# Attention in groups of 64 keys over two pairs of heads, all in 64x64 tiles, with part of the queries and keys turned by VectorE

## The chip, the cores and the metric

The kernel runs on one core of a Trainium2 chip. The metric is the device time of one execution in microseconds; the time before is the median of three runs.

The engines are called as the profile calls them: PE is TensorE's matmuls and PEld its weight loads, DVE is VectorE, ACT is ScalarE, POOL is GpSimd and SP is SyncE, which here issues most DMAs.

## The reference

The kernel computes a normalized attention and, on its output, an MLP mixer. All is float32 but the mixer's weights, which arrive as float64. Cut to what matters:

```python
# q, k, v: (8, 12, 448, 64)
q_n = q / sqrt(mean(q*q, -1) + 1e-6) * g_q        # k_n likewise, with g_k
scores = q_n @ k_n.T / sqrt(64)
attn = exp(scores - max(scores))
attn = attn / (sum(attn) + 1e-9)
x = heads_side_by_side(attn @ v)                   # (8, 448, 768)
h = relu(x.T @ w_tok1) @ w_tok2                    # 448 -> 256 -> 448, over tokens
u = x + h.T
out = u + relu(u @ w_ch1) @ w_ch2                  # 768 -> 1536 -> 768, over channels
```

## The kernel before

**Elements and pairs.** The batch has eight elements of twelve heads. Two heads make a pair `p`; an element has six pairs (`NPAIR`), and there are 48 in all. A pair fills 128 partitions: one head in rows 0 to 63 and the other in rows 64 to 127.

**One program order.** Every engine executes its instructions in the order in which the Python code emits them. That order is made by `merge` (L27), which interleaves lists of (cost, function) items so that each list advances at the same share of its total cost. An item of cost 0.0 is placed as soon as its list's turn comes, and occupies no share. While the mixer of element `b` runs (`tok1`, `tok2`, `ch1`, `ch2`), the attention of element `b + 1` is merged into it. Element 0's attention runs first, merged with the conversion of the mixer's weights to float32 (`weight_items`), most of which VectorE does. Element 0's mixer uses plain products (`ch1_first`, `ch2_first`, L713 and L731); the other elements use seven products in place of eight per block of the channel matmuls (`ch1` L750, `ch2` L807). These seven products combine block sums of the operands, and the sums of the weights are made once, by `sum_items`.

**Steps of the attention.** `att_step(g)` emits one step; four steps, s = 0 to 3, take two pairs `p` and `p + 1` through. A step's attention matmuls are one item (`tiled`), about which the other items of the step are placed.

- `score` (L321) takes a chunk of 128 keys of one pair. Two matmuls with a 64x128 stationary tile, one per head, lie in the upper and the lower half of the array.
- `score_last` (L335) takes the last 64 keys of both pairs in four 64x64 tiles. 448 keys are three chunks of 128 and this one.
- ScalarE then takes the exponential (L311). The factor of the key's norm is the activation's per-partition scale, so that only queries have to be scaled beforehand.
- `av` (L422) multiplies a chunk by the values, with 128x64 tiles, and `av_last` (L434) does it for the last keys in 64x64 tiles.
- The softmax sums: for element 0, matmuls with a matrix of ones (`ones`, L401) accompany each chunk. From element 1 on, `chunk_sums` adds the chunks up first (the first sum on POOL, L382; the others on VectorE, L388 and L393), and `row_sums` makes one pass of `ones` per pair.
- `denominator` turns the sums, takes the reciprocal, turns back and scales the output (L463 to L469, all VectorE).

**Preparing queries and keys.** `load_qk` (L1034, L1036, L1040) loads a pair into one of three buffers of `qk_t` (element 0's go to a larger area). `squares` (ScalarE L1057, VectorE L1061 and L1065) and `roots` with `rsqrt` (VectorE, L1090 to L1095) give the reciprocal norms, `swap` (L346) copies one of them to the other half of the partitions, and `scale` (L291) scales the queries, on VectorE for elements 0 and 1 and on POOL after that. `trans_qk` turns queries and keys by TensorE (L301, four transposes each) and ScalarE multiplies by g while copying out of PSUM (L303). The keys of a pair p + 4 are loaded at step 1 of pair p, those of p + 5 at step 3; their squares follow at steps 0 and 1 of pair p + 2.

**Buffers.** PSUM has four buffers for scores, transposes and row sums (`ps_S`), two for attention outputs (`ps_O`) and two for the mixer's products (`ps_M`, called m_ps). `e_pool` has four buffers for exponentials, `es_pool` one for their sums, `qkT_pool` two for turned pairs, `unit_pool` six for units of mixer weights, which SP loads in the order of use (L676).

Of the kernel before, what the change touches and what calls it, by code (L numbers as in the profile page):

```python
# [8 lines left out]
F32 = mybir.dt.float32  # L9
# [35 lines left out]
def whole(ctx, tc, shifted, pre, q, k, v, g_q, g_k, moe_w_tok1, moe_w_tok2, moe_w_ch1, moe_w_ch2, out):  # L45
# [11 lines left out]
    NS = 4  # L57
# [13 lines left out]
    K3 = NS - 1  # L71
    assert S == K3 * P + D and NPAIR % 2 == 0
# [7 lines left out]
    pre.st_pool = pool("st_pool", 4)  # L80
    pre.nt_pool = pool("nt_pool", 2)
    qkT_pool = pool("qkT_pool", 2)
# [181 lines left out]

    def heads(p):
        return pre.heads(p)

    def load_v(p):
        b, hs = heads(p)
        st["v", p] = vt = pre.v_t[p % 2]  # L270
        nc.sync.dma_start(
            out=vt[:, 0:2 * K3 * D].rearrange("p (h f) -> p h f", h=2),
            in_=v[b, hs, 0:K3 * P].rearrange("h (p c) d -> p h (c d)", c=K3))
        for a in range(2):
            nc.sync.dma_start(out=vt[last_rows(p, a), 2 * K3 * D:], in_=v[b, hs][a][K3 * P:S])

    def last_rows(p, a):

        return slice((a ^ p % 2) * D, (a ^ p % 2) * D + D)

    def scale(p, eng=nc.gpsimd):

        n = 2 * NS
        qk, rs = st["qk", p], st["rs", p]
        parts = [(R, 0, n, rs[0:R, 0:n].unsqueeze(2))]
        if shifted:
            parts.append((P, n, n - 2, rs[:, n:2 * n - 2].unsqueeze(2)))
            parts.append((P, 2 * n - 2, 2, rs[:, 2 * n - 2:2 * n - 1].unsqueeze(2)))
        for rows, o, m, r in parts:
            x = qk[0:rows, o * D:(o + m) * D].rearrange("p (r d) -> p r d", d=D)  # L290
            eng.tensor_tensor(out=x, in0=x, in1=r.to_broadcast([rows, m, D]), op=ALU.mult)  # L291

    def trans_qk(p, i):
        qk = st["qk", p]
        if ("qkT", p) not in st:
            st["qkT", p] = qkT_pool.tile([P, S + NS * P], F32, name="qkT")
        ps = s_tile("t_ps")
        n = P if i else R
        for c in range(NS):
            o = (i * NS + c) * P  # L300
            nc.tensor.transpose(ps[:, c * n:(c + 1) * n], qk[0:n, o:o + P], ident[0:n, 0:n])  # L301
        to = st["qkT", p][:, S:S + NS * P] if i else st["qkT", p][:, 0:S]
        nc.scalar.mul(to, ps[:, 0:NS * n], g_t[:, i:i + 1])  # L303
        if p and i == 1 or p == 0 and i == 0:
            st.pop(("qk", p))
# [4 lines left out]
    def exp(out, ps, p, r):  # L310
        nc.scalar.activation(  # L311
            out=out, in_=ps[:, 0:S], func=AF.Exp, scale=st["rs", p][:, r:r + 1])

    def score(p, kc):

        qkT = st["qkT", p]
        e = st["e", p, kc] = e_tile()
        pss = [s_tile("s_ps") for a in range(2)]
        for a in range(2):
            o = S + kc * P  # L320
            nc.tensor.matmul(  # L321
                out=pss[a][:, 0:S], lhsT=qkT[a * D:(a + 1) * D, o:o + P],
                rhs=qkT[a * D:(a + 1) * D, 0:S], start=True, stop=True)
        for a in range(2):
            exp(e[:, a, :], pss[a], p, 2 * NS + kc * 2 + a)

    def score_last(p):

        e = e_tile()
        pss = [s_tile("s_ps") for i in range(2)]  # L330
        for i in range(2):
            qkT = st["qkT", p + i]
            for a in range(2):
                o = S + K3 * P + a * D
                nc.tensor.matmul(  # L335
                    out=pss[i][last_rows(p + i, a), 0:S], lhsT=qkT[a * D:(a + 1) * D, o:o + D],
                    rhs=qkT[a * D:(a + 1) * D, 0:S], start=True, stop=True)
        for i in range(2):
            exp(e[:, i, :], pss[i], p + i, 4 * NS - 2 + i)
            st["e", p + i, K3] = e  # L340

    def swap(p):

        rs = st["rs", p]
        for a in range(2):
            nc.vector.tensor_copy(  # L346
                out=rs[last_rows(p, a), 4 * NS - 1:4 * NS], in_=rs[a * D:(a + 1) * D, 4 * NS - 2:4 * NS - 1])

    def score_shifted(p):

        qT, kT = st["qkT", p][:, 0:S], st["qkT", p][:, S:S + NS * P]
        for kc in range(NS):
            st["e", p, kc] = e_tile()
        for c in range(NS):
            for a in range(2):
                ps = s_tile("s_ps")
                last = K3 * P + a * D
                for o, k in ((0, kT[a * D:(a + 1) * D, 0:K3 * P]), (K3 * P, kT[a * D:(a + 1) * D, last:last + D])):
                    nc.tensor.matmul(
                        out=ps[0:R, o:o + k.shape[-1]], lhsT=qT[a * D:(a + 1) * D, c * R:(c + 1) * R],  # L360
                        rhs=k, start=True, stop=True)
# [5 lines left out]
                pt = s_tile("p_ps")  # L367
                r = last_rows(p, a)
                for kc in range(NS):

                    k = eq[0:R, kc * P - (r.start if kc == K3 else 0):min(S, (kc + 1) * P)]
                    nc.tensor.transpose(pt[0:k.shape[-1], kc * R:(kc + 1) * R], k, ident[0:R, 0:R])
                for kc in range(NS):
# [791 lines left out]
```

## Time and profile before

| what | value |
|---|---|
| median of 3 runs | 1432.62 us (1427.3 to 1433.27) |
| the profiled execution, its own time | 1438.43 us |
| its span in the profile | 1436.3 us |
| PE busy | 1368.3 us, 95% |
| DVE busy | 726.7 us, 51% |
| ACT busy | 431.2 us, 30% |
| POOL busy | 423.6 us, 29% |
| mean share of the DMA queue q1 / q10 | 56.6% / 5.1% |
| mean granted clock of TensorE | 0.978 |

Busy times come from one profiled execution, so sums are made against its own time, 1438.43 us, and not against the median. A row of the timeline gives the start in us from the start of the span, the duration in us, engine, line, operation, what is written and read, shapes and the number of records merged into the row. Matmuls are pipelined: a row's duration reaches into the next one's, and the time that a group costs is the difference between its start and the next group's start. A number in brackets is idle time of the engine, with what ended it.

### The profile page before, as it was taken

To read this page: it belongs to the slowest core of one execution; us is meant where nothing else is said; L and a number is where in the kernel's file an instruction comes from. 1 tells how busy PE (TensorE), PEld (TensorE's weight loads), DVE (VectorE), ACT (ScalarE), POOL (GpSimd) and SP (SyncE) were. 2 spreads that over 40 slices of the span, in tenths; PEclk is the share of its full clock that TensorE was granted. 3 is DMA by queue.
4 is the path that set the end of the run, shared out by engine and by line. 5 is a ranking of instruction groups with operands and counts; after the bars stand their busy time and mean duration, and the time that the engine had idled before them with its cause. 6 is when DMAs were issued, how large, how long until landed. Compare 5 with 4: busy or idle time off the path is not lost.

```text
span 1436.3 us, 18872 instructions
## 1 busy us (share of the span) xinstructions
PE 1368.3 (95%) x6472; PEld 960.4 (67%) x6472; DVE 726.7 (51%) x1336; ACT 431.2 (30%) x779; POOL 423.6 (29%) x425
## 2 busy tenths in 40 slices
PE   6988996999999999999999999999999999999997
PEld 2333442446776867785777867786777857876997
DVE  7779888225463355644445354633556444432312
ACT  5565453203432043312333033312333134310100
POOL 1122323336664033221233123421323123311320
PEclk9899998999999999999999999999999999999999
DMA  7557777785887934666456744667356744457455
GB/s 176 142 178 201 221 206 181 201 217 141 233 260 219 225 95 136 169 159 156 130 142 177 184 112 133 152 185 173 101 146 177 179 114 142 130 144 172 144 175 119
DMA packets 408301, 238.76 MB, mean 166 GB/s; under 512 B 274500, under 2 KB 366788, under 8 KB 408196
## 3 DMA queue, kind: packets, MB, share of 16 engines
q1 hardware_dynamic: 318178, 226.24, 56.6%
q10 hardware_dynamic: 89890, 11.22, 5.1%
q8 instruction: 54, 0.88, 0.3%
q14 instruction: 51, 0.42, 0.1%
q0 software_dynamic: 128, 0.00, 0.0%
HBM read 197.85 MB, written 39.52 MB: 165 GB/s over the span
## 4 chain that ended last, share of the span: by engine, by line
PE 77%; DMA 7%; DVE 5%; issue 1%; SPq 1%; ACT 1%; ACTq 1%; POOL 0%; DVEq 0%; POOLq 0%
PE m_ps L750 24%; PE m_ps L807 20%; PE s_ps L321 7%; PE o_ps L422 7%; PE m_ps L628 5%; PE m_ps L620 3%; DMA unit<-ws 3%; PE m_ps L731 3%; PE d_ps L401 2%; PE t_ps L301 2%; PE m_ps L713 2%; DMA out_dram<-turned 1%; DMA xs<-turned 1%; PE o_ps L434 1%; DVE raw L213 1%
## 5 line engine op out<-in xcount | busy, mean ns | idle before, releaser
L807 PE MATMUL m_ps<-hb,unit 128*128 128x224 f32 x1764 | 347.1, 356 | 6.8 <-DMA unit<-ws 6.8
L807 PEld LDWEIGHTS m_ps<-hb,unit 128*128 128x128 f32 x1764 | 332.0, 191 | 23.5 <-issue 11.3
L311 ACT ACTIVATE e<-s_ps,rs 128x448 f32<-128x448 f32 x336 | 186.9, 634 | 195.2 <-PE s_ps L321 163.0
L750 PE MATMUL m_ps<-tu,unit 128*128 128x224 f32 x1008 | 202.9, 355 | 0.0
L750 PEld LDWEIGHTS m_ps<-tu,unit 128*128 128x128 f32 x1008 | 187.5, 190 | 16.2 <-issue 4.9
L750 PE MATMUL m_ps<-uT,unit 128*128 128x224 f32 x756 | 152.8, 355 | 0.0
L321 PE MATMUL s_ps<-qkT 64*128 64x448 f32 x576 | 142.8, 595 | 7.8 <-ACT qkT L303 5.7
L750 PEld LDWEIGHTS m_ps<-uT,unit 128*128 128x128 f32 x756 | 141.2, 190 | 13.1 <-issue 12.2
L422 PE MATMUL o_ps<-e,v 128*64 128x448 f32 x576 | 132.3, 563 | 0.0
L816 POOL TENSOR_TENSOR uT<-uT,r 128x448 f32<-128x448 f32 (+1 forms) x56 | 52.7, 952 | 235.9 <-DVE r L816 140.5
L388 DVE TENSOR_TENSOR es<-es,e 128x896 f32<-128x896 f32 x42 | 53.2, 1268 | 117.4 <-ACT e L311 74.6
L463 DVE STREAM_TRANSPOSE dt<-d_ps 128x448 f32<-128x448 f32 x42 | 27.3, 650 | 168.0 <-PE d_ps L401 168.0
L291 POOL TENSOR_TENSOR qk_t<-qk_t,rs 112x512 f32<-112x512 f32 x36 | 37.4, 1060 | 226.1 <-DVE rs L1095 166.1
L321 PEld LDWEIGHTS s_ps<-qkT 64*128 64x128 f32 x576 | 51.3, 193 | 74.9 <-issue 57.6
L382 POOL TENSOR_TENSOR es<-e 128x896 f32<-128x896 f32 x42 | 89.8, 2138 | 32.5 <-ACT sq L1057 29.0
L816 DVE TENSOR_TENSOR uT<-uT,m_ps 128x448 f32<-128x448 f32 (+1 forms) x70 | 34.1, 503 | 124.8 <-PE m_ps L807 124.8
L620 PE MATMUL m_ps<-x,w_sb 112*128 112x384 f32 x256 | 90.9, 508 | 5.6 <-DMA x<-xs 3.4
L303 ACT ACTIVATE qkT<-t_ps,g_t 128x448 f32<-128x448 f32 (+1 forms) x96 | 60.2, 661 | 109.9 <-PE t_ps L301 109.9
L422 PEld LDWEIGHTS o_ps<-e,v 128*64 128x64 f32 x576 | 33.1, 137 | 87.4 <-issue 85.8
L246 POOL TENSOR_TENSOR stage<-raw 128x512 f32<-128x512 f32 x36 | 41.4, 1151 | 146.6 <-DVE raw L232 78.8
L628 PE MATMUL m_ps<-w_sb,h 128*128 128x448 f32 x192 | 78.5, 558 | 4.8 <-DVE uT L633 4.8
L620 PEld LDWEIGHTS m_ps<-x,w_sb 112*128 112x128 f32 x256 | 49.4, 197 | 42.9 <-issue 11.1
(92 smaller groups left out, 1491.8 us busy)
## 6 DMA issues: line engine op xcount, KB each, us to landing
unit<-ws SPq DMA_DIRECT2D x318, 384.0 KB, 3.5
raw<-in_moe_w_ch_dram SPq DMA_DIRECT2D x72, 256.0 KB, 3.3
out_dram<-turned ACTq DMA_DIRECT2D x192, 56.0 KB, 3.4
qk_t<-in_q_dram SPq DMA_DIRECT2D x84, 112.0 KB, 3.5
xs<-turned SPq DMA_DIRECT2D x168, 56.0 KB, 2.3
x<-xs SPq DMA_DIRECT2D x14, 672.0 KB, 6.3
v<-in_v_dram SPq DMA_DIRECT2D x48, 192.0 KB, 2.8
ws<-stage SPq DMA_DIRECT2D x36, 256.0 KB, 3.7
```

The lines of the kernel that those rows point to most:

```text
L303: nc.scalar.mul(to, ps[:, 0:NS * n], g_t[:, i:i + 1])
L311: nc.scalar.activation(out=out, in_=ps[:, 0:S], func=AF.Exp, scale=st["rs", p][:, r:r + 1])
L321: nc.tensor.matmul(out=pss[a][:, 0:S], lhsT=qkT[a * D:(a + 1) * D, o:o + P], rhs=qkT[a * D:(a + 1) * D, 0:S], start=True, stop=True)
L382: nc.gpsimd.tensor_tensor(out=es[:], in0=st["e", p, 0][:], in1=st["e", p, 1][:], op=ALU.add)
L388: nc.vector.tensor_tensor(out=es[:], in0=es[:], in1=st["e", p, 2][:], op=ALU.add)
L422: nc.tensor.matmul(out=o[a * D:(a + 1) * D, 0:S], lhsT=vt[:, c:c + D], rhs=e[:, a, :], start=start, stop=stop)
L620: nc.tensor.matmul(out=ps[:, 0:HC], lhsT=w1_sb[0:R, c, jc * P:(jc + 1) * P], rhs=st["x", h][0:R, c, :], start=(c == 0), stop=(c == NS - 1))
L628: nc.tensor.matmul(out=ps[:, 0:S], lhsT=st["h1", jc][:, cc * P:(cc + 1) * P], rhs=w2_sb[:, jc].rearrange("p c r -> p (c r)"), start=(jc == ...
L731: nc.tensor.matmul(out=ps[:, 0:S], lhsT=w, rhs=natural(half)[:, :, t, :], start=(half == 0 and t == 0), stop=(half == 1 and t == KF - 1))
L750: nc.tensor.matmul(out=ps[:, j * HS:(j + 1) * HS], lhsT=w[:, t, j, :], rhs=m, start=(t == 0), stop=(t == KC - 1))
L807: nc.tensor.matmul(out=ps[:, j * HS:(j + 1) * HS], lhsT=st["w"](j, t), rhs=hb[:, HB[what], t, :], start=(t == 0), stop=(t == KF - 1))
L816: add = lambda e, o, x, y: e.tensor_tensor(out=o, in0=x, in1=y, op=ALU.add)
```

## The change

Scores, values and softmax sums of both pairs now all go by groups of 64 keys (seven groups, `NK`). Each group is four 64x64 matmuls, one for each head of the two pairs, in the four tiles of the array; `rows_of` gives the half of the partitions for a head. The four steps take the groups (0), (1, 2), (3, 4), (5, 6) for the scores; the values follow one step later, so that the last two groups of two pairs are multiplied at step 0 of the next two, where `row_sums` and both `denominator` calls now stand together.

`scale` now scales queries and keys, always on VectorE, and the exponential has no scale operand any more. The two vectors g are multiplied into one, which goes to the queries alone.

For elements 0 and 1 (`plain`), TensorE still turns queries and keys. From pair 12 on, `load_qk` loads blocks of 32 rows by 32 columns, 128 bytes at a time, to where VectorE's 32x32 stream transpose turns them in place (`turn_qk`); ScalarE then only multiplies the queries by g. A head's two halves of 32 columns then lie in different quarters of the partitions, so `roots` adds the two half sums, with four copies across quarters.

`qk_t` has two buffers in place of three, `qkT_pool` three in place of two, and the values three in place of two and another for pair 0. A pair is loaded one step before its squares. The memsets of zeros, `swap` and L1065 are gone. In element 0's mixer the last three items are now merged too.

```diff
     def load_v(p):
...
         for a in range(2):
-            nc.sync.dma_start(out=vt[last_rows(p, a), 2 * K3 * D:], in_=v[b, hs][a][K3 * P:S])
+            nc.sync.dma_start(
+                out=vt[rows_of(p, a)].rearrange("r (k d) -> r k d", d=D),
+                in_=v[b, hs][a].rearrange("(k r) d -> r k d", r=D))
...
+    def scale(p):
+        x, d = pre.by_rows(p, st["qk", p])
+        r = st.pop(("rs", p))
+        nc.vector.tensor_tensor(out=x, in0=x, in1=r.unsqueeze(2).to_broadcast(list(x.shape)), op=ALU.mult)
...
+    def turn_qk(p, i):
...
+        if pre.plain(p):
+            ps = s_tile("t_ps")
+            for c in range(NS):
+                o = (i * NS + c) * P
+                nc.tensor.transpose(ps[:, c * R:(c + 1) * R], qk[0:R, o:o + P], ident[0:R, 0:R])
+            src = ps[:, 0:S]
+        else:
+            nc.vector.transpose(out=to, in_=qk[:, i * S:(i + 1) * S])
+            src = to
+        if i == 0:
+            nc.scalar.mul(to, src, g_t[:, 0:1])
+        elif pre.plain(p):
+            nc.scalar.copy(out=to, in_=src)
...
+    def score(t, k):
+        e = st["e", t, k] = e_tile()
         pss = [s_tile("s_ps") for i in range(2)]
         for i in range(2):
-            qkT = st["qkT", p + i]
+            qkT = st["qkT", 2 * t + i]
             for a in range(2):
+                h = slice(a * D, a * D + D)
                 nc.tensor.matmul(
+                    out=pss[i][rows_of(i, a), 0:S], lhsT=qkT[h, 1, k * D:(k + 1) * D], rhs=qkT[h, 0, :],
+                    start=True, stop=True)
         for i in range(2):
+            nc.scalar.activation(out=e[:, i, :], in_=pss[i][:, 0:S], func=AF.Exp)
...
+    def group_sums(t, k):
+        if k == 1:
+            st["es", t] = es_pool.tile([P, 2, S], F32, name="es")
+        es = st["es", t]
+        eng = nc.gpsimd if k < 3 else nc.vector
+        eng.tensor_tensor(out=es[:], in0=(es if k > 1 else st["e", t, 0])[:], in1=st["e", t, k][:], op=ALU.add)
...
+    def row_sums(t):
+        es = st.pop(("es", t))
+        for p in (2 * t, 2 * t + 1):
+            st["d", p] = s_tile("d_ps")
+            ones(p, es[:, p % 2, :], start=True, stop=True)
...
+        def finish():
+            if s == 0 and t:
+                last = (p - 2, p - 1)
+                for k in (NK - 2, NK - 1):
+                    values(last, k)
+            if live:
+                for k in ((0,), (1, 2), (3, 4), (5, 6))[s]:
+                    score(t, k)
+            if s == 0 and t:
+                if not on_pe(p - 1):
+                    row_sums(t - 1)
+                for i in last:
+                    denominator(i)
...
+        items.append((2.4 if s == 1 else 3.2, tiled))
+        if live and not on_pe(p):
+            items += [(0.5, lambda k=k: group_sums(t, k)) for k in ((), (1, 2), (3, 4), (5, 6))[s]]
+        if s == 0 and 3 < p + 1 < NP:
+            items.append((0.0, lambda: load_v(p + 1)))
+        if live and s == 1 and 3 < p + 2 < NP:
+            items.append((0.0, lambda: load_v(p + 2)))
+        if live and s in (3, 0):
+            j = p + 4 if s == 3 else p + 3
+            if pre.first_slot + 2 <= j < NP:
+                items.append((0.0, lambda: pre.load_qk(j, st)))
...
+        if turned and not inside:
+            items += [(0.4 * pre.plain(q), lambda i=i: turn_qk(q, i)) for i in (1, 0)]
...
-        for _, fn in merge(att, early[:-3]) + early[-3:] + last_items(b, sums[6:12]):
+        tail = 3 if b else 0
+        for _, fn in merge(att, early[:len(early) - tail]) + early[len(early) - tail:] + last_items(b, sums[6:12]):
...
     def load_qk(self, p, st, other=None):
...
+            S = self.R * NS
+            for m in range(4):
+                o = 32 * m % D
+                eng.dma_start(
+                    out=qk[32 * m:32 * m + 32, i * S:(i + 1) * S].rearrange("t (n c) -> t n c", c=32),
+                    in_=x[b, hs][32 * m // D][:, o:o + 32].rearrange("(n t) c -> t n c", t=32))
...
     def roots(self, p, pairs, st):
...
+        if not self.plain(p):
+            t = self.nt_pool.tile([128, 56], F32, name="nt")[:, 0:2 * n]
+            for m in range(4):
+                nc.vector.tensor_copy(out=t[32 * m:32 * m + 32], in_=x[32 * (m ^ 1):32 * (m ^ 1) + 32])
+            nc.vector.scalar_tensor_tensor(
+                out=x, in0=x, scalar=self.D * 1e-6, in1=t, op0=ALU.add, op1=ALU.add)
+        self.rsqrt(rs, x)
```

## The prediction

> **What bounds the kernel now.** I read the page's totals first, then busy time by stretch, then TensorE's timeline at the attention, then VectorE's.
>
> ```profile
> span 1436.3 us, 18872 instructions
> PE 1368.3 (95%) x6472; PEld 960.4 (67%) x6472; DVE 726.7 (51%) x1336; ACT 431.2 (30%) x779; POOL 423.6 (29%) x425
> ```
> ```profile
> 0.00:330.00 330.00, 281.56 (x1028) 124.89 (x1028) 224.62 (x408) 143.04 (x253) 86.09 (x96) 0.93 0.71 192
> 330.00:1280.00 950.00, 942.23 (x4742) 703.22 (x4740) 460.35 (x851) 276.63 (x504) 309.40 (x299) 1.00 0.60 160
> 1280.00:1436.00 156.00, 144.55 (x706) 132.29 (x704) 41.77 (x77) 11.57 (x22) 28.11 (x30) 0.97 0.57 151
> ```
>
> The columns after the stretch are its length and the busy time of PE, weight loads, DVE, ACT, POOL, then clock, DMA share and GB/s. From 330 to 1280 us TensorE is busy 99% at full clock and VectorE 48%: time taken off TensorE there shortens the kernel one for one. That stretch holds the attention of elements 2 to 7 (36 of 48 pairs of heads). Before 330 us TensorE idles 48 us, and from 108 to 252 us VectorE is the fuller engine (125.7 of 144 us against 121.5): TensorE's savings there are worth little. After 1280 us no attention is left.
>
> Next, what attention costs on TensorE, from start to next start. A float32 matmul shows as two records, so x8 in 64x64 form is four matmuls.
>
> ```profile
> 713.84 0.99 PE L301 MATMUL t_ps<-ident,qk_t 112*128 112x112 f32 x8
> 714.66 2.44 PE L750 MATMUL m_ps<-tu,unit 128*128 128x224 f32 x12
> 717.03 0.98 PE L335 MATMUL s_ps<-qkT 64*64 64x448 f32 x8
> 717.94 1.02 PE L321 MATMUL s_ps<-qkT 64*128 64x448 f32 x4
> 718.89 0.97 PE L422 MATMUL o_ps<-e,v 128*64 128x448 f32 x4
> 719.80 4.81 PE L750 MATMUL m_ps<-tu,unit 128*128 128x224 f32 x24
> ...
> 726.80 1.77 PE L321 MATMUL s_ps<-qkT 64*128 64x448 f32 x8
> 728.51 0.98 PE L434 MATMUL o_ps<-e,v 64*64 64x448 f32 x8
> 729.42 0.97 PE L422 MATMUL o_ps<-e,v 128*64 128x448 f32 x4
> 730.22 0.92 PE L401 MATMUL d_ps<-es,one_c 128*64 128x448 f32 x4
> 731.08 1.21 PE L750 MATMUL m_ps<-tu,unit 128*128 128x224 f32 x5
> ```
>
> Two row tiles with two key chunks take 728.51 - 726.80 = 1.71 us, with one chunk 0.95: a pass over the whole array is 0.76, leaving the 64x128 form costs 0.20. L422 and L401 together take 1.66 = two passes of 0.75 and 0.15 to leave 128x64. A 64x64 pass takes 0.91, 0.16 of it the change of form. The eight transposes of a pair take 0.82. Do 64x64 passes follow each other without loss? Element 0 shows it:
>
> ```profile
> 84.85 0.98 PE L434 MATMUL o_ps<-e,v 64*64 64x448 f32 x8
> 85.66 0.93 PE L401 MATMUL m_ps<-e,one_c 64*64 64x448 f32 x8
> 86.52 0.97 PE L422 MATMUL o_ps<-e,v 128*64 128x448 f32 x4
> ```
>
> Two passes in 1.67 = 2 x 0.75 + 0.16. Last, VectorE's softmax denominator, 2.2 us a pair:
>
> ```profile
> 701.97 0.65 DVE L463 STREAM_TRANSPOSE dt<-d_ps 128x448 f32<-128x448 f32 x1 [5.76 <-PE d_ps L401]
> 702.65 0.24 DVE L465 RECIPROCAL rc<-dt 128x14 f32<-128x14 f32 x1
> 702.93 0.65 DVE L467 STREAM_TRANSPOSE rd<-rc 128x448 f32<-128x448 f32 x1
> 703.61 0.62 DVE L469 TENSOR_TENSOR uT<-o_ps,rd 128x448 f32<-128x448 f32 x1
> ```
>
> **The Trainium skill.** "TensorEngine Tiling (Array Packing)", Key Properties, says that changing the tiling mode drains TensorE; the 0.15 to 0.20 us above agree. "TensorE: Matmul & The Clock Gate", Part 3, says that tiles run at once, some 4 ns apart; the full-rate 64x64 passes above agree. The same page (architectural detail) says that VectorE and ScalarE are strict FIFOs: a long group on VectorE holds back every PSUM drain behind it. "VectorE: DVE Perf Modes", errata section, prices a float32 tensor_tensor at (N+151)/0.96 ns: 0.69 us at N = 512 (L291 on VectorE measures 0.689) and, for widths not seen, 1.09 us at 896 and 1.22 at 1024.
>
> **The change, part by part.** A cycle is four attention steps (two pairs of heads).
>
> (a) Transposes. From pair 12 on eight TensorE transposes a pair go: 36 x 0.82 = 29.5 us, on the bound.
>
> (b) Row sums. From element 1 on L401 took a 128x64 pass per pair; in the new layout both pairs' sums fit one 64x64 pass. One pass of 0.75 goes per cycle; 18 cycles in the saturated stretch: 13.5 us.
>
> (c) Forms. Scores and values keep 7 + 7 passes a cycle. Changes of form before: steps 0 and 1 cost 0.20 + 0.15 each, steps 2 and 3 0.20 + 0.16 + 0.15 each, 1.72 in all. After, each step is one 64x64 block: 4 x 0.16 = 0.64. 18 x 1.08 = 19.4 us.
>
> Sum in the stretch: 62.4 us. Element 1's three cycles hold 3 x (0.75 + 1.08) = 5.5 more; TensorE waits there part of the time (its longest gap, 14.0 us before L731, waits for converted weights), so I take half, 2.7. Element 0 computes its sums on TensorE as before; its form changes are covered by VectorE and ScalarE: nothing.
>
> (d) VectorE, each pair from 12 on: two stream transposes 1.30 (L463's duration), scaling queries and keys 1.09 (from POOL, which loses 36 x 1.06 = 37 us and isn't late), wider root chain and half-row exchange about 0.5; gone are swap, L1065 and part of the reduction, 0.5. Net 2.4 x 36 = 87 us. Group sums: 4 x 1.09 for 2 x 1.09 + 4 x 0.62 a cycle, 6 us less in all. Early pairs: keys scaled too, 0.53 each, about balanced by swap and L1065. VectorE goes to some 810 us, 58% of the new span: no bound as a sum. But groups get longer. In step 0 two denominators come together, 4.4 us; in step 1 reduction 1.09, exchange 0.8, roots 2.1, two scalings 2.2: 6.2 us, and ScalarE's square (1 us) ahead of it. m_ps has two buffers and a product takes 2.33 us, so TensorE goes on for two products, 4.7 us, plus an attention step (2.4 to 3.2) if one falls between. In step 0 a drain comes 4.4 + 0.6 + 0.2 = 5.2 us late against 4.7: 0.5 lost. In step 1 some 7.8 against 4.7 to 7.9: 0 to 3.1. Five of seven products are drained by VectorE. I take 0.85 us a cycle, 18 x 0.85 = 15 us.
>
> (e) Loads. Eight DMAs a pair instead of six for q and k, two instead of three for v: SP's issue time is about equal (0.5 us each). 3584 packets of 128 bytes for 1280; at the 13 ns that the ACT queue's 89890 packets show (5.1% of 16 engines' span) at most 67 us over 16 engines, 5 points on a DMA share of 60%: hidden. But the load now comes one step ahead of the square that reads it, not two or three. Issue 8 x 0.5 plus landing 3.5 (the longest 9.5) is 7.5 us; step starts lie 9 to 17 us apart. It mostly fits: nothing in the forecast; up to 3 us a cycle for the range.
>
> (f) ScalarE loses the key copy, POOL the scaling and memsets: neither is on the path. Exponentials lose their scale operand, not their 0.63 us.
>
> (g) The start. The first scores need both pairs turned: VectorE's chain for pair 1 (reduction, roots, scaling, 4.7 us) now precedes them, so TensorE starts some 5 us later than 11.9. VectorE itself reaches its first conversion about 2 us earlier (17.5 now; one root chain less) and SP has less to issue. Bounds -3 to +6; I take +2. Moving element 0's last items into the merge: nothing, its successor waits for a DMA.
>
> Sum: 62.4 + 2.7 - 15 - 2 = 48 us. The profiled execution took 1438.4 us (span 1436.3), 5.8 over the median 1432.6: 1390 for it, **1384.6** for the median.
>
> **The rivals.**
>
> *No give-back* (20%): the merge puts every long group beside an attention step. For it: VectorE's step-1 group of 3.7 us stalls nothing now. 1432.6 - 65 + 2 = 1370.
>
> *Late loads* (15%): squares wait for q and k, ScalarE and VectorE queue behind them, 2.2 us a cycle in all: 40 back, 1410. For it: SP waits 211 us in all for L750's release of unit buffers, and the new loads queue behind. Against: one step usually suffices.
>
> *Instruction issue* (7%): eight short instructions a pass outrun the sequencer. The TensorE page (Part 1) gives some 62 ns per matmul without hardware decode; four make 248 ns, under the half pass of 376, but with four weight loads at the same rate 496. A pass is then 0.99, 15 passes x 0.24 x 18 = 65 us: 1434, no change. Against: the passes at 84.85.
>
> *Slower* (14%): VectorE's queue sets m_ps. If the step-1 group falls where no attention step follows within two products, the drain is done 0.7 + 7.2 + 0.6 = 8.5 us after a product's end, needed at 4.7: 3.8 lost, with step 0's 0.5 4.3 a cycle, 18 x 4.3 = 77: 1432.6 - 63 + 77 = 1447. It decides from 63 / 18 = 3.5 us a cycle. Against: VectorE idles half the stretch and the items lie midway between steps.
>
> That the tiles don't run at once at all is excluded by the lines at 717.03 and 84.85.
>
> **The numbers.** The forecast case has 44%. Own range of the faster cases: 1364 to 1425. The range reaches up to the issue case, 1436, and leaves out the slower one and the far edges, under 2 in 10. About 0.5% is what a measurement tells from no change here. Faster: 44 + 20 + 15 = 79%; same 7%; slower 14%.
>
> **What would show it.** In 330 to 1230 us: no t_ps on TensorE after element 1, d_ps one 64x64 pass a cycle, attention steps of 2.4 to 3.2 us without 64x128 or 128x64 forms, DVE near 60%, TensorE at 95% or more. Wrong if passes take over 0.8 us inside a block (issue), or if TensorE or L750 and L807 wait for VectorE's drains over 3.5 us a cycle (slower), or ACT's square for q and k loads (late loads).

## The result, and the profile after

The changed kernel takes **1447.28 us** (median of 4 runs, 1447.1 to 1452.82) beside 1432.94 for the kernel before on the same chip (4 runs, 1427.3 to 1436.66). The ratio is 1.0113, with a 95% interval of 1.0072 to 1.0154: slower by 0.7 to 1.5%, where 1384.6 was forecast. The profiled execution took 1447.23 us, with a span of 1445.3.

The page's totals:

```profile
span 1445.3 us, 20543 instructions
PE 1306.8 (90%) x7408; PEld 933.5 (65%) x7408; DVE 783.0 (54%) x1382; ACT 368.6 (26%) x707; POOL 394.1 (27%) x385
```

TensorE's busy time fell by 61.5 us (from 1368.3), close to the 65 that were worked out, and the span rose all the same. So TensorE now idles where it did not. The stretch that was saturated shows it (columns as before: length, then busy time of PE, weight loads, DVE, ACT and POOL, clock, DMA share, GB/s):

```profile
330.00:1280.00 950.00, 890.17 (x5239) 671.72 (x5241) 516.01 (x929) 225.09 (x436) 279.29 (x264) 0.98 0.64 159
```

TensorE is at 94% where it was at 99%; VectorE went from 460 to 516 us and is far from full. The attention itself is what was forecast:

```profile
716.07 0.93 PE L375 MATMUL d_ps<-es,one_c 64*64 64x448 f32 x8
716.93 2.54 PE L695 MATMUL m_ps<-uT,unit 128*128 128x224 f32 x12
...
721.67 1.73 PE L321 MATMUL s_ps<-qkT 64*64 64x448 f32 x16
723.22 0.93 PE L395 MATMUL o_ps<-e,v 64*64 64x448 f32 x8
724.08 4.81 PE L695 MATMUL m_ps<-uT,unit 128*128 128x224 f32 x24
```

Row sums of two pairs take one pass (L375), no transpose of queries or keys stands on TensorE, and a step of three passes takes 724.08 - 721.67 = 2.41 us, that is 3 x 0.75 and one change of form of 0.16. What TensorE waits for has changed (columns: total us, times, longest):

```profile
PE m_ps L752 <- DMA unit<-ws: 33.7, 11, 16.0
PE m_ps L573 <- DVE uT L578: 21.5, 7, 5.1
PE t_ps L298 <- DVE hb L286: 19.0, 2, 12.6
PE m_ps L676 <- DMA unit<-ws: 16.4, 1, 16.4
```

In the kernel before:

```profile
PE m_ps L731 <- DMA unit<-ws: 14.0, 1, 14.0
PE m_ps L807 <- DMA unit<-ws: 6.8, 7, 2.4
...
PE m_ps L628 <- DVE uT L633: 4.8, 3, 4.2
```

L752 is the second channel product, which reads the units of weights (L807 before), and L676 is the same for element 0 (L731 before, so most of its wait isn't new). L573 is tok2 (L628 before), L298 the transposes of the first pairs. Waits for units went from 20.8 to 50.1 us. One wait isn't there: before the squares of the pairs from 12 on ScalarE stands idle 0.1 us in all.

To see where in the span the time lies I take the starts of each element's first tok1 product as marks. An element in the table is its mixer, beside which the next element's attention runs:

| part | forecast, us | measured, after less before |
|---|---|---|
| up to element 0's tok1 (104.8 before) | +2 | +12.8 |
| elements 0 and 1, up to 490.7 before | -10.6 | +4.1 |
| elements 2 to 6, up to 1307.7 before | -39.5 | -5.6 |
| the rest | 0 | -2.3 |
| sum | -48 | +9.0 |

(The forecast's 62.4 - 15 = 47.4 us belong to 18 cycles; 15 of them lie in the third row. The second row has the other three, 7.9 us, and element 1's 2.7.) Against the forecast, loss is in every row but the last, and most of it in the third. The profiled execution of the kernel before lies 5.5 us above its median, that of the changed kernel on its median: the +9.0 stands for 14.3 between the medians.

### The profile page after: what moved, and what is told of

It reads as the page before. It is cut to its first block, busy times and chain, and to the rows that moved or that the text cites. A ratio compares the mean times of both kernels' runs of the same rounds, so it can differ in the third digit from the quotient of the medians.

```text
span 1445.3 us, 20543 instructions
## 1 busy us (share of the span) xinstructions
PE 1306.8 (90%) x7408; PEld 933.5 (65%) x7408; DVE 783.0 (54%) x1382; ACT 368.6 (26%) x707; POOL 394.1 (27%) x385
## 4 chain that ended last, share of the span: by engine, by line
PE 66%; DVE 11%; DMA 11%; issue 3%; SPq 2%; ACT 1%; ACTq 1%; POOL 1%; DVEq 0%; POOLq 0%
PE m_ps L695 21%; PE m_ps L752 19%; PE o_ps L395 7%; PE s_ps L321 6%; DMA unit<-ws 4%; PE m_ps L573 4%; DMA out_dram<-turned 4%; PE m_ps L565 3%; PE m_ps L676 2%; PE m_ps L658 2%; DVE qk_t L286 2%; ACTq L529 1%; DMA ws<-raw 1%; DVE raw L214 1%; SPq L529 1%
## 5 line engine op out<-in xcount | busy, mean ns | idle before, releaser
L752 PE MATMUL m_ps<-hb,unit 128*128 128x224 f32 x1764 | 349.3, 359 | 35.2 <-DMA unit<-ws 33.7
L752 PEld LDWEIGHTS m_ps<-hb,unit 128*128 128x128 f32 x1764 | 336.2, 193 | 53.6 <-issue 33.6
L325 ACT ACTIVATE e<-s_ps 128x448 f32<-128x448 f32 x336 | 156.4, 547 | 199.0 <-PE s_ps L321 199.0
L395 PE MATMUL o_ps<-e,v 64*64 64x448 f32 x1316 | 153.1, 547 | 6.6 <-DVE uT L428 5.7
L321 PE MATMUL s_ps<-qkT 64*64 64x448 f32 x1260 | 144.0, 550 | 0.5 <-ACT x L548 0.5
L573 PE MATMUL m_ps<-w_sb,h 128*128 128x448 f32 x192 | 86.4, 600 | 23.3 <-DVE uT L578 21.5
L363 DVE TENSOR_TENSOR es<-es,e 128x896 f32<-128x896 f32 x84 | 97.7, 1164 | 4.7 <-ACT e L325 2.2
L395 PEld LDWEIGHTS o_ps<-e,v 64*64 64x64 f32 x1316 | 49.4, 134 | 78.3 <-issue 66.3
L304 ACT ACTIVATE qkT<-qkT,g_t 128x448 f32<-128x448 f32 x36 | 24.1, 669 | 261.7 <-DVE qkT L301 261.7
L321 PEld LDWEIGHTS s_ps<-qkT 64*64 64x64 f32 x1260 | 44.0, 133 | 68.8 <-issue 59.5
L363 POOL TENSOR_TENSOR es<-e 128x896 f32<-128x896 f32 x21 | 44.7, 2126 | 159.3 <-ACT e L325 159.3
L578 DVE TENSOR_TENSOR uT<-uT,m_ps 128x448 f32<-128x448 f32 x48 | 29.3, 616 | 103.0 <-PE m_ps L573 103.0
L573 PEld LDWEIGHTS m_ps<-w_sb,h 128*128 128x128 f32 x192 | 38.5, 210 | 68.8 <-issue 29.7
```

The costliest lines, as they stand in the source:

```text
L321: nc.tensor.matmul(out=pss[i][rows_of(i, a), 0:S], lhsT=qkT[h, 1, k * D:(k + 1) * D], rhs=qkT[h, 0, :], start=True, stop=True)
L325: nc.scalar.activation(out=e[:, i, :], in_=pss[i][:, 0:S], func=AF.Exp)
L363: eng.tensor_tensor(out=es[:], in0=(es if k > 1 else st["e", t, 0])[:], in1=st["e", t, k][:], op=ALU.add)
L395: nc.tensor.matmul(out=st["o", p][a * D:(a + 1) * D, 0:S], lhsT=vt[rows, k * D:(k + 1) * D], rhs=e[rows, :], **kw)
L573: nc.tensor.matmul(out=ps[:, 0:S], lhsT=st["h1", jc][:, cc * P:(cc + 1) * P], rhs=w2_sb[:, jc].rearrange("p c r -> p (c r)"), start=(jc == ...
L578: nc.vector.tensor_tensor(out=uT, in0=uT, in1=ps[:, 0:S], op=ALU.add)
```

## Two waits, read from the profile

**Weight units.** TensorE waits 2.77 us at 776.65, and SP's queue says why. Columns: start, length, queue, line, transfer, number of DMAs.

```profile
750.08 4.56 SPq L621 DMA_DIRECT2D unit<-ws  x3
755.98 0.86 SPq L983 DMA_DIRECT2D qk_t<-in_q_dram  x2
758.24 1.28 SPq L274 DMA_DIRECT2D v<-in_v_dram  x2
759.57 1.13 SPq L983 DMA_DIRECT2D qk_t<-in_q_dram  x2
760.75 2.05 SPq L983 DMA_DIRECT2D qk_t<-in_k_dram  x4
765.76 7.12 SPq L529 DMA_DIRECT2D xs<-turned  x12
772.93 0.97 SPq L621 DMA_DIRECT2D unit<-ws  x2
```
```profile
776.65 4.82 PE L752 MATMUL m_ps<-hb,unit 128*128 128x224 f32 x12 [2.77 <-DMA unit<-ws]
```

From 754.6 to 772.9 us, 18.3 us long, SP issues no unit: eight loads of a pair's queries and keys, two of v and the twelve sends of x stand in one run of 22. The next unit, issued at 772.9, lands some 3.6 us later, and TensorE goes on at 776.65. Of the 18.3 us, 12.4 are the issues themselves; the rest are waits between them. Such a run comes once in each of elements 2 to 5 (17.4 to 18.3 us without a unit). In the kernel before the loads of a pair lay behind the sends, with a unit between:

```profile
755.69 6.20 SPq L584 DMA_DIRECT2D xs<-turned  x12
761.99 0.44 SPq L676 DMA_DIRECT2D unit<-ws  x1
762.54 0.37 SPq L1034 DMA_DIRECT2D qk_t<-in_q_dram  x1
...
764.45 1.24 SPq L1036 DMA_DIRECT2D qk_t<-in_k_dram  x2
765.74 1.25 SPq L1040 DMA_DIRECT2D qk_t<-in_k_dram  x2
767.09 12.68 SPq L676 DMA_DIRECT2D unit<-ws  x6
```

The two long waits, in elements 0 and 1, have a longer run ahead of them, in which the transfers of the weights' conversion stand as well. Ahead of the 16.0 us that end at 442.8, SP issues no unit from 408.4 to 433.4 (39 issues of other transfers); ahead of the 16.4 us that end at 251.6, none from 210.4 to 248.3 (49). Only the first is new: the kernel before waits 14.0 us at the place of the second, with no unit issued from 201.4 to 237.2. And the late issue is not all of the first: TensorE goes on only 9.4 us after SP issues a unit again, where the median of all units is 3.6 us from issue to landing.

**VectorE's group in tok2.** VectorE and TensorE around 860 us:

```profile
852.91 1.77 DVE L1027 COPY nt<-ms 32x56 f32<-32x56 f32 x4
...
857.45 2.09 DVE L286 TENSOR_TENSOR qk_t<-qk_t,rs 128x896 f32<-128x896 f32 x2
859.47 0.61 DVE L578 TENSOR_TENSOR uT<-uT,m_ps 128x448 f32<-128x448 f32 x1
```
```profile
855.74 1.68 PE L395 MATMUL o_ps<-e,v 64*64 64x448 f32 x16
860.13 6.09 PE L573 MATMUL m_ps<-w_sb,h 128*128 128x448 f32 x11 [2.71 <-DVE uT L578]
```

Reduction, exchange, roots and two scalings run from 851.79 to 859.5 without a pause; the drain of a tok2 product (L578) stands behind them. A tok2 product takes 1.5 us (four records of 0.376), so two buffers carry TensorE 3 us and not the 4.7 of the forecast's products.

Part of the group's length comes from POOL. The four copies of the exchange (L1027) take 1.77 us here and 0.81 in the next such group, at 898.14. Here the first of them alone takes 1.12 us and ends at 854.03, as a sum on POOL ends, at 853.99:

```profile
851.91 2.08 POOL L363 TENSOR_TENSOR es<-es,e 128x896 f32<-128x896 f32 x1
```

No run takes this 0.96 us out by itself.

The stall costs twice: after it the clock falls.

```profile
860.00:862.00 2.00, 1.87 (x4) 0.95 (x5) 1.64 (x4) 0.00 (x0) 1.40 (x2) 0.81 0.00 0
862.00:863.50 1.50, 1.50 (x3) 0.69 (x3) 0.99 (x3) 0.00 (x0) 0.32 (x1) 0.50 0.00 0
```

The granted clock is the third number from the end: 0.50. Four records of L573 stand 0.75 us apart there instead of 0.376, some 1.5 us more. The Trainium skill, "TensorE: Matmul & The Clock Gate", section "Why this matters for your kernels", asks for no idle gaps over about 3 us; here one of 2.71 was enough. Its length alone doesn't decide: in the run q_pool (below) a gap of 2.71 us too, from 827.58 to 830.29, is followed by full clock. In all 17 traces the granted clock changes only at times that lie whole multiples of 3.413 us apart, a fixed grid. The changed kernel's gap has 2.31 us in one interval of its grid, that of q_pool at most 1.73. Of 6207 such intervals at full clock (from 120 us on, without the last 15 us), all 126 with 2.01 us or more without a matmul were followed by half clock, and only 3 of the 6063 with less than 1.85 us; between the two it went both ways.

## The experiments

All are edits of the changed kernel, but for before_pool. Each was run 4 to 19 times and has its ratio to the kernel before, run on the same chip, with the 95% interval.

| run | edit | median us | ratio |
|---|---|---|---|
| qk_pool | q and k loads on POOL's queue | 1419.05 | 0.9907 (0.9888 to 0.9926) |
| qk_act | the same on ACT's queue | 1475.71 | 1.0286 (1.0244 to 1.0329) |
| scale_late | each scaling ahead of its own turn | 1435.12 | 1.0008 (0.9988 to 1.0029) |
| turn_pe | all pairs turned by TensorE | 1418.68 | 0.9897 (0.9867 to 0.9927) |
| both | qk_pool and scale_late | 1400.98 | 0.9761 (0.9728 to 0.9794) |
| all3 | both and joint | 1397.45 | 0.9744 (0.9707 to 0.9782) |
| joint | start in one group | 1442.36 | 1.0054 (1.0034 to 1.0075) |
| before_pool | kernel before, its loads on POOL | 1436.97 | 1.0020 (1.0001 to 1.0038) |
| k_pool | only k loads on POOL | 1413.88 | 0.9871 (0.9842 to 0.9900) |
| q_pool | only q loads on POOL | 1405.50 | 0.9796 (0.9769 to 0.9823) |
| plain18 | all3, element 2 turned by TensorE | 1395.04 | 0.9736 (0.9713 to 0.9758) |
| pe_late | turn_pe and scale_late | 1565.80 | 1.0926 (1.0897 to 1.0954) |
| send_pool | sends of x on POOL's queue | 1414.29 | 0.9868 (0.9833 to 0.9904) |
| start_free | pairs 0 and 1 not scaled | 1441.08 | 1.0054 (1.0038 to 1.0071) |
| best | plain18, but only q loads on POOL | 1395.49 | 0.9732 (0.9698 to 0.9766) |

### First: SP's queue, VectorE's group, or VectorE's sum

**qk_pool** and, with `nc.scalar` instead, **qk_act**:

```diff
-                eng.dma_start(
+                self.nc.gpsimd.dma_start(
                     out=qk[32 * m:32 * m + 32, ...
```

Expected of qk_pool:

> One edit to the changed kernel: the eight loads of queries and keys per pair from pair 12 on are issued on POOL's queue, not on SP's. Theory A (SP's in-order queue makes mixer units late: the 16.0 us gap at 442.8 us and the two waits of L752 for units in each later element): the 16 us gap shrinks to what it was before (about 3 us) and L752's waits for units go; with their half-clock stretches that is 13 + 5 x 4.5 = 35 us less, about 1412 us. The gaps at L573 (2.7 us per element, waiting for VectorE) stay. Theory B (VectorE's long group in step 1 is the main cause): under 10 us less, 1438 to 1447. Rival C (the DMA engines' 128-byte packets delay the units, whoever issues them): L752's waits stay as they are and the time too.

Expected of qk_act:

> The same loads issued on ACT's queue. Theory A: the same gain at the unit loads as on POOL's queue (35 us), less what ScalarE loses by issuing 288 DMAs at about 0.5 us each, 24 us per element, and by waiting for the transposes that free the buffer: exponentials come later, so 1412 to 1435. Theory B: 1438 or more. Rival C: no gain, 1447 or more.

qk_pool gave 28 us back, some 7 fewer than theory A expected, and TensorE's waits of 16 us at 252 and 443 us fell to at most 0.7 and to 1.6. The 128-byte packets are the same there, so by themselves they don't delay the units (rival C). On ACT's queue the same edit lost another 28. That is outside theory A's range; the open ranges of B and C hold it by number, but the trace shows another cause. ACT's timeline of that run, around one pair's loads, and TensorE's longest new wait:

```profile
455.83 6.35 ACTq L983 DMA_DIRECT2D qk_t<-in_k_dram  x4
462.23 0.95 ACT L1000 ACTIVATE sq<-qk_t 128x896 f32<-128x896 f32 x1 [10.42 <-DMA qk_t<-in_k_dram]
```
```profile
PE s_ps L321 <- ACT qkT L304: 28.4, 8, 9.9
```

ACT does nothing for 10.42 us while its queue holds the issues of four loads, spread over 6.35, and the gain of queries (L304) that TensorE's scores need stands in the same queue. The Trainium skill, "TensorE: Matmul & The Clock Gate", Part 1 (architectural detail), calls ScalarE a strict FIFO; the run agrees, with the square at 462.23 directly behind the last issue. Which queue takes the loads decides the sign.

**scale_late**, for pairs from 12 on:

```diff
-            items += [(0.3 * (n < NPAIR), lambda i=i: scale(n + i)) for i in range(2)]
+            if pre.plain(n):
+                items += [(0.3 * (n < NPAIR), lambda i=i: scale(n + i)) for i in range(2)]
+        if turned and not pre.plain(q):
+            items.append((0.0, lambda: scale(q)))
```

> One edit to the changed kernel: from pair 12 on, a pair is scaled by VectorE right before it is turned (steps 2 and 3), not in step 1. VectorE's work is the same; its step-1 group is shorter by two scalings, 2.2 us of about 7.7. Theory B: the gaps at L573 shrink from 2.7 us by about 2.2, and the half-clock stretches of 3.4 us that follow them go: 6 elements x (2.2 + 1.7 + some) = 20 to 25 us less, 1422 to 1428. Theory A: the unit gap at 442.8 and L752's waits stay; alone, A expects no change beyond 5 us. Rival D (VectorE's total, 783 us, is the limit, however it is ordered): no change.

It gave 12 us, half of what theory B expected: the waits of tok2 for VectorE are gone from the later elements, those for units stay (29.2 us at L755, which is L752 moved by three lines). With the same work on VectorE in two groups these waits are gone, so it was the length of the group and not VectorE's sum.

**turn_pe**: `plain` returns True for every pair.

> One part of the change undone: all pairs are loaded in rows of 256 bytes (four DMAs a pair in place of eight) and turned by TensorE; groups of 64 keys, loads one step ahead and scaling on VectorE in step 1 stay. TensorE does 36 x 0.77 = 28 us more. Theory A: four issues a pair fewer on SP (2 us per pair, 12 us per element), so the gap at 442.8 shrinks by half or more and L752's waits go: minus 30. Theory B: the step-1 group loses the four copies and part of the root chain (2.0 us of 7.7) and gains 0.3 in scaling: gaps at L573 of about 1 us: minus 10 to 15. Together 1430 to 1440; if only the transposes counted, 1447 + 28 = 1475.

It puts 34.0 us of transposes back on TensorE between 330 and 1280 us, and is 28.6 us faster than the changed kernel, where 7 to 17 were expected. With four loads a pair and no wait in SP's queue for VectorE's turn, the unit waits are gone (0.2 us in all). As it stands, the turn by VectorE costs more than it brings.

### Second: do the causes add, and was it so before

**both** joins the two edits. **joint** works on pairs 0 and 1 at the start:

```diff
             self.squares(0, self.st)
-            self.roots(0, 1, self.st)
+            self.squares(1, self.st)
+            ms = self.st.pop(("ms", 1))
+            self.rsqrt(rs_0, ms.rearrange("p a n -> p (a n)"))
...
     scale(0)
+    scale(1)
     turn_qk(0, 1)
```

**all3** is all of it. **before_pool** makes qk_pool's edit in the kernel before.

both:

> The two edits together: the 128-byte loads of queries and keys are issued on POOL's queue (theory A, SP's queue is late with the weight units), and the scaling of a pair stands ahead of its own turn instead of in one group with the roots (theory B, VectorE's group outlasts the two buffers of tok2). If A and B are two separate causes, their gains add: 1419 (A alone) less 12 (B alone gave 1435 from 1447) is 1407 us, 1403 to 1412, with no wait over 1 us at L573 for VectorE's uT and at most one wait of 1.5 us a layer element at L752 for a unit. If they are one cause (VectorE's late turn holds the loads, so either cure does the same), the sum is not reached: 1415 to 1420.

all3:

> As the run before, and the start in one group: the squares of pairs 0 and 1 together, one chain of roots for both, both scalings, then the turns. Theory S (the serial chains of pair 0 and pair 1 make the start late): the first score comes at about 17.5 us where it stood at 22.4, the gap of 12.6 us gets longer by some 3 us while those that follow (6.4, 2.6, 4.5) shrink by more, and all later marks move by 4 to 6 us: 1401 to 1405 us. Rival: the start is set by the loads of queries, keys and values and by the two denominators at once (5.3 us at 61 us), which take the gain back before 105 us: 1406 to 1410, no change to the run before.

joint:

> Only the start in one group, nothing else changed. Theory S: the mark of the first tok1 product moves from 117.6 us to 112 to 114, and the end with it, 1441 to 1444. Rival: the mark stays within 1 us, 1446 to 1449. If the mark moves and the end does not, the wait for the weight units at 251 us (16 us) takes it up: units are set by SP's queue, not by TensorE.

before_pool:

> The kernel BEFORE with one edit: its loads of queries and keys (six a pair, from pair 12) are issued on POOL's queue instead of SP's. It asks whether theory A is a matter of the change alone. In the kernel before TensorE waited 7 us over its nominal steps in four elements, and 14.0 us for a unit at 243 us. If SP's queue was as good as full before, and the change only made it worse: the 14 us go and some of the 7, 1414 to 1422 us. If the queue had room before and only the change's two more loads a pair and their wait for the turn filled it: 1430 to 1435, as before. If POOL's own work holds the issues (it scales the keys there): slower, over 1440.

both came to 1401, below the sum of 1407 and below its whole range: two causes, whose gains together are more than their sum. Why more, no run shows; qk_pool alone still has 7.4 us of waits for units after 500 us, both has 4.1. In that kernel TensorE's stretch is nearly full again, at 97%:

```profile
330.00:1280.00 950.00, 922.22 (x5468) 704.95 (x5469) 529.41 (x953) 225.70 (x436) 446.13 (x520) 0.99 0.67 167
```

joint moved the first mark from 117.6 to 114.5 and the end by 5 us; in all3 it moved the end by 3.5, less than the runs of either kernel spread (1391.91 to 1402.64 for all3), and all3 as a whole came below both its ranges. before_pool gained nothing, 1437: SP's queue had room before, and the gain of qk_pool belongs to the change.

But this does not fit a theory of numbers. SP issues 430 loads of queries, keys and values in both kernels: from pair 12 on nine DMAs a pair became ten, and the pairs before have fewer. Summed, these issues take 236 us before and 242 after. Six us over eight elements are no reason for forty.

### Third: number, wait, or order

**k_pool** and **q_pool** each take one half of the loads from SP (`self.nc.gpsimd if i else eng`, and the reverse).

k_pool:

> Of each later pair only the four loads of keys are issued on POOL's queue; the four of queries stay on SP's, where the first of them waits until the pair two before has been turned. It splits theory A in two. If the number of issues delays the weight units (eight a pair at some 0.48 us), half of them are gone and about half or more of the 28 us: 1424 to 1434 us, the same as the next run. If the wait in the queue for the turn delays them, it is still there: 1440 to 1447.

q_pool:

> The counterpart: only the four loads of queries are issued on POOL's queue, the four of keys stay on SP's. The keys of a pair are turned first, so these loads wait about one turn (some 1.1 us) less. By number: 1424 to 1434 us, as the run before. By the wait: clearly better than the run before, 1422 to 1432 against 1440 to 1447, with SP's wait for the turn well below the 42.9 us of the changed kernel.

Both were better than expected by number, and better than qk_pool. The wait for the turn is refuted as the cause by itself: q_pool's SP still waits for it about as long as the changed kernel's (42.9 us there):

```profile
SPq L983 <- DVE qkT L301: 41.4, 23, 3.7
```
```profile
PE m_ps L573 <- DVE uT L578: 12.0, 5, 2.7
PE m_ps L695 <- DVE r L700: 2.3, 5, 0.5
...
PE m_ps L752 <- DMA unit<-ws: 0.2, 1, 0.2
```

The second fence is TensorE's waits of q_pool from 500 us on: 0.2 us for units, where the changed kernel has 17.7 there. (Before 500 us q_pool keeps more: 3.1 us at 240 and 11.2 at 435.) What both runs lack from 500 us on is the run of 22: their longest is the twelve sends alone. **send_pool** breaks it from the other end and leaves every load on SP:

```diff
-        send(nc.sync, turn(b, j), xs[:, o:o + P])
+        send(nc.gpsimd, turn(b, j), xs[:, o:o + P])
```

> The changed kernel with one edit: the sends of the turned x (12 an element in one run, 168 in all) are issued on POOL's queue; all loads of queries, keys and values stay on SP's. If the run of 22 issues in SP's order is what makes the weight units late, breaking it from its other end does as well as taking half of the loads away: 1408 to 1422 us, with no stretch over 12 us without a unit outside the window of tok1 and tok2. If it is the loads' own wait for the turn or their bytes in the DMA engines, the waits at L752 stay: 1438 to 1447. If POOL is too late with the sends: a longer wait for x at L565, over 1447.

1414.29, within what was expected of the order. After 437 us no wait for a unit over 1 us is left on TensorE (17.5 us of them stand before), though two of SP's stretches without a unit are longer than was expected, 17.5 us from 401 and 12.9 from 459; waits of L752 for VectorE's results (5.9 us) and some that the profile puts down to nothing (4.6) stand there instead. Of the three readings the order is the one left: not how many transfers SP issues (as many before as after, and qk_pool, which takes 288 loads away, gains least of these four runs), but how many stand in one run ahead of a unit that TensorE needs. The timeline at 776.65 shows it at work. But each of the four runs also takes 144 to 288 issues off SP; none changes the order alone, with every issue left on SP's queue. What stays open is why q_pool beats k_pool by 8 us and qk_pool by 14; POOL is busy 570 us in qk_pool and 481 in the other two, which explains no difference between those two.

**pe_late** was to price the turn by VectorE without the two waits.

> All pairs turned by TensorE from 256-byte loads on SP's queue, as in the run that did so, and with it each later pair's scaling ahead of its own turn. Beside the kernel with both edits (1401 us, turned by VectorE, loads on POOL's queue) it tells what the turn on VectorE is worth once both waits are gone. If TensorE's transposes are on the path to the full (36 x 0.82 us = 29.5 us, as predicted): 1425 to 1431. If the late scaling is worth 10 to 12 us here too: 1406 to 1410, and the turn on VectorE only some 5 to 9. If the late scaling gives nothing here, 1417 to 1420.

It missed all three, with 1565.80. The transposes stand on TensorE directly behind the scaling that they now wait for:

```profile
727.95 0.96 PE L298 MATMUL t_ps<-ident,qk_t 112*128 112x112 f32 x8 [2.49 <-issue]
```
```profile
725.63 1.08 DVE L363 TENSOR_TENSOR es<-es,e 128x896 f32<-128x896 f32 x1
726.64 1.21 DVE L286 TENSOR_TENSOR qk_t<-qk_t,rs 112x1024 f32<-112x1024 f32 x1
```

TensorE stops until the scaling ends at 727.85, behind a group sum in VectorE's queue; such waits of L298, which the profile puts down to nothing, come to 92.0 us in all. With VectorE's turn the same late scaling holds back nobody, since the turn follows it on the same engine. So it says nothing of the price asked for. q_pool and turn_pe, both with four such loads a pair on SP, stand 13 us apart in favour of VectorE's turn, but they differ in more than the turn.

**plain18**: all3, with `p < 3 * self.NPAIR` in `plain`.

> The kernel with all three edits (loads on POOL's queue, late scaling, start in one group), and one element more whose queries and keys are turned by TensorE from 256-byte loads: those of element 2, which are loaded and turned while element 1 is mixed and the weights are still being converted. Element 1's stretch is 191.7 us there, 12 more than in the kernel before. If the loads on POOL's queue hold up POOL's part of the conversion (so that TensorE waits at L695's VectorE results and for v), the stretch falls to 180 to 184 us less the price of six pairs' transposes on TensorE, some 5 us: 1388 to 1393 us in all. If these waits have another cause, only the price is left: 1400 to 1404.

1395.04, between the two. Element 1's stretch fell by 10.1 us, but element 0's rose by 8.9. The two together are 376.4 (qk_pool), 376.0 (q_pool), 374.6 (both), 373.8 (all3) and 372.6 (plain18) with 385.9 before. What one of the two gains the other loses, by a cause that no run isolates: they are to be read as one, and as one they are near the forecast's -10.6.

### Last: the start, and one kernel of all

**start_free** leaves pairs 0 and 1 unscaled. **best** is plain18 with q_pool's division of the loads.

start_free:

> The changed kernel, but the queries and keys of the first two pairs are not scaled by their roots (this part of the computation is left out; their squares and roots are still worked out, and a constant takes the gain's place). So TensorE's first transposes wait for the loads alone. If the chain squares, roots, scaling ahead of the turn makes the start late: the first score comes at 10 to 14 us where it stood at 22.4, the first tok1 mark at 106 to 109 where it stood at 117.6, and the end is 8 to 11 us earlier, 1436 to 1440. If the start is set by the loads or by the attention's own chain of exp, values and denominators: the mark stays at 114 or later, and the end within 3 us of 1447.

best:

> What the runs point to in one kernel: queries of later pairs loaded on POOL's queue and keys on SP's (1405 alone against 1419 with both on POOL's), each later pair scaled ahead of its own turn, the start in one group, and element 2 too turned by TensorE. If the gain of dividing the loads (14 us) adds to the kernel with the other three (1395): 1381 to 1388. If that gain was the same wait that the other edits have already removed: 1392 to 1398.

TensorE's first lines, of the changed kernel and then of start_free:

```profile
12.62 1.73 PE L298 MATMUL t_ps<-ident,hb 112*128 112x112 f32 x8 [12.62 <-DVE hb L286]
20.72 1.75 PE L298 MATMUL t_ps<-ident,hb 112*128 112x112 f32 x8 [6.38 <-DVE hb L286]
22.41 3.79 PE L321 MATMUL s_ps<-hb 64*64 64x448 f32 x22
```
```profile
9.34 4.51 PE L323 MATMUL s_ps<-hb 64*64 64x448 f32 x24
...
22.64 3.68 PE L323 MATMUL s_ps<-hb 64*64 64x448 f32 x16 [7.28 <-ACT e L327]
```

In the changed kernel ScalarE squares pair 1 only after it has copied pair 0's turned tiles, and VectorE's second chain ends at 20.7. Without the chains the first score comes 13 us earlier, but the first mark only 6.0 (111.6) and the end 6, between what the two theories expected: half of it is lost at once to a wait for exponentials. The chain is about half of the late start. The other half was not taken apart. It may be the attention's own order in element 0, with no product beside it: waits of 5.3 us for two denominators at once and of 8.6 ahead of transposes stand in the changed kernel and in every edit of it, and not in the kernel before.

best came to 1395.49 us, level with plain18 and all3 within what these runs can tell (its own runs spread from 1385.98 to 1399.21). A further gain from dividing the loads is not seen, as expected if the other edits had already removed the same wait.

## Why the prediction was wrong

- **(a), (b), (c), TensorE's work: right.** 65 us were to go, 61.5 went, and the forms and passes are as worked out. The instruction-issue rival is refuted by the block of 2.41 us.
- **(d), VectorE: right in size, wrong in place.** VectorE went to 783 us (some 810 forecast; the sums that the change replaced were priced at 1.09 and 0.62 us, where the profile before has 1.27 and 0.84 in the mean, L388 and L393). The give-back of 15 us compares with 12 that scale_late recovered. It falls not on each cycle's products but once an element on tok2, where a buffer is worth 1.5 us and not 2.33. The exchange takes the 0.8 us of the forecast where POOL doesn't hold it, and 1.77 at 852.91, beside one of POOL's group sums.
- **(e), loads: the step that failed.** "SP's issue time is about equal" holds (236 and 242 us), and so does "it mostly fits", of the squares. Nothing followed from either, because the step asked only who waits for the new loads and not who is queued behind them. q_pool, which takes four loads of each later pair off SP, is 41.8 us faster than the change; send_pool 33.0 with all of them there. That is two thirds and a half, respectively, of the 62.7 us between forecast and result.
- **(g), the start: mis-sized.** +2 was taken with bounds up to +6; it is 12.8. The second chain is not 4.7 us of VectorE alone: ScalarE's squares stand ahead of it, behind pair 0's copies, and scores come 10.5 us later instead of 5. start_free, without the chains, has half of the delay at the first mark; the cause of the other half stays open.
- **Elements 0 and 1**: -10.6 forecast, +4.1 measured, -9.9 in q_pool and -8.6 in send_pool. They lost by (e) as well.
- **The rivals.** Late loads named SP's queue but had the squares wait; the queue hurt in the other direction. The slower rival had the right number, 1447, by the wrong cause: TensorE's waits at L573 for VectorE come to 10.2 us in the twelve cycles from 667 to 1319 us, under 1 us a cycle where it needed 3.5.

With the order mended, the scaling spread and the start in one group, all3 comes near the forecast: +9.4, -12.1, -42.1 and -1.4 in the four rows of the table, 1391.91 us in its profiled execution where 1390 was forecast. Part of that is luck: this execution is the fastest of all3's four, and the one of the kernel before is on the slow side. By the medians all3 gains 36.7 us (1397.45 beside 1434.12), of the 48 forecast.

## What to carry to other kernels

A step that moves transfers is priced twice: by who waits for them, and by what stands behind them in the issuing engine's queue. Totals of issue time don't show that; look for the longest run of issues between two that a bound engine needs. When VectorE gets longer groups, hold them against the shortest product beside which they can fall, not against the usual one.

## What the runs showed of the hardware

- An issue on POOL's queue keeps POOL itself busy 0.635 us (288 of them: 181 us in the groups of POOL of the kernel both), against about 0.5 of SP's queue. The Trainium skill, "Trainium Kernel Development and Optimization", section "Key Constraints", says that issuing from several engines saves only the sequencer's issue time. The runs don't contradict that, and show what a place in the queue can be worth: 42 us of 1447 in q_pool.
- A copy of 32 x 56 elements from one quarter of the partitions to another takes 0.18 us on VectorE, where an operation on 128 x 56 in place takes 0.22. But beside an elementwise operation of POOL it can last until that one ends: of the changed kernel's 72 copies (L1027), the 37 with none beside them took 0.18 to 0.19 us, and all 24 that took longer, 0.35 to 2.00 us, had one beside them. The reductions of 128 x 896 ahead of them (L1001) took 1.08 us in the median both with POOL at work when they started (21 of them) and without (15); VectorE's sums L595 took 0.39 us without and 0.73 with.
- Whether a gap on TensorE was followed by half clock (3.41 us or more of it) went by how much of it fell into one interval of a 3.413 us grid: from 2.01 us on always, under 1.85 us almost never (126 of 126 and 3 of 6063 intervals in the 17 traces).
